# Second level of Strassen's algorithm in the first GEMM of a retention and ELU kernel, with sums taken into evacuations and twenty sums a block on GpSimd

## The chip, the cores and the metric

The kernel runs on one core of a Trainium2 chip. The metric is the device time of one execution in microseconds (us). A profile is of one execution, and its span is about 2 us below the time of that same execution. The profiled execution of the kernel before took 660.89 us, 2.8 us less than its median. Engines in the profile are PE (TensorE), PEld (its weight loads), DVE (VectorE), ACT (ScalarE), POOL (GpSimd) and SP (SyncE). Tiles lie in SBUF; TensorE's products are written to banks of PSUM, and an evacuation takes a result out of PSUM.

## The reference, cut to what matters

```python
# retention: 4 sequences of 768 tokens, 8 heads of 64; cut: k, v, decay
y = retention(q, k, v)                           # 3072 tokens x 512
h = x @ w_in                                     # 512 -> 2048: the first GEMM
g = np.where(h > 0.0, h, np.exp(np.minimum(h, 0.0)) - 1.0)   # ELU
out = g @ w_out                                  # 2048 -> 512: the second GEMM
```

Everything is float32. The 3072 tokens are done in six blocks of 512, counted from 0. While the second GEMM of one block runs, the retention of the next block is computed beside it.

## The kernel before

Strassen's algorithm (in Winograd's form) replaces the eight products of a 2x2 block multiplication by seven, at the price of sums of blocks. One level of it, as it is written in this kernel:

```python
    def strassen(product, use, between):
        # (cut: the yields, at which the caller interleaves other work)
        pa = bank("a")
        product(1, pa, True)
        m1 = kept(pa)                       # an evacuation from PSUM to SBUF
        pb = bank("b")
        product(2, pb, True)
        use("C11", plus(pb, m1))
        product(6, pa, False)               # adds to what stands in pa
        u2 = kept(pa)
        pd = bank("d")
        product(7, pd, True)
        product(5, pa, False)
        u4 = kept(pa)
        use("C22", plus(pd, u4))
        product(3, pa, False)
        use("C12", pa)
        product(4, pd, False)
        use("C21", plus(pd, u2))
```

The first GEMM uses one level in each of four groups of columns of `w_in` (`first(n)`, 7 products of 256 columns each). Each of its results goes through the ELU: two activations on ScalarE into a tile `r`, then one instruction on VectorE. Behind it VectorE takes the sums T3 and T1, which are inputs of the second GEMM:

```python
    def elu(g, h):
        r = epool.tile([P, 512], FP32, name="r", tag="r")
        nc.scalar.activation(r, h, AF.Relu, scale=-1.0)
        nc.scalar.activation(r, r, AF.Exp, scale=-1.0)
        flush()
        later.append(lambda: nc.vector.scalar_tensor_tensor(g, r, -1.0, h, ALU.add, ALU.max))
    # in first(n), behind the ELU of C12:
                later.append(lambda: sub(mine("T3"), mine("C22"), mine("C12")))
                later.append(lambda: sub(mine("T1"), mine("C12"), mine("C11")))
```

The second GEMM has had two levels from block 2 on (`second_twice`): 49 products of 128 columns. Each of its seven outer products needs four input sums of 128x512, on VectorE:

```python
        def inputs(j):
            ...
            sub(t[:, 0], b12, b11)
            sub(t[:, 1], b22, t[:, 0])
            sub(t[:, 2], b22, b12)
            sub(t[:, 3], b21, t[:, 1])
```

`ts` in the profile is a tile of such sums, `gC` and `gT` are quarters of the ELU's results and their sums, `wq` is the ring of small weights for the second level, and `res` holds the results of one inner product of the second GEMM.

## Time and profile before

| | before |
|---|---|
| time, median of 4 runs | 663.67 us (661.65 to 663.89) |
| span of the profiled run | 658.9 us |
| TensorE busy, clock granted | 637.3 us (97%), 1.000 |
| VectorE busy | 434.7 us (66%) |
| GpSimd busy | 23.8 us (4%) |
| start of block 2; blocks 2, 3, 4; block 5 to the end | 251.6; 101.65, 102.66, 102.87; 100.1 us |

### The profile page before, as it was taken

The page shows a single profiled execution, that of the slowest core. Times are in us where ns is not written, and L with a number is a line of the kernel's source. Part 1 is how long each engine was busy: PE and PEld are TensorE (multiplying, and loading weights), DVE is VectorE, ACT ScalarE, POOL GpSimd, SP SyncE. Part 2 cuts the span into 40 slices and gives each one's busy share as a digit, 9 for nine tenths or more (in the row PEclk, how much of TensorE's full clock was granted, in tenths as well). Part 3 has the DMA queues.
Part 4 walks back from the last instruction along what each step waited for, and adds up shares of the span by engine and source line. Part 5 has one row for each costly group of instructions (what it writes and reads, how often), then busy time and mean ns, then how long its engine had stood idle before and what let it go on. Part 6 is the DMA issues. An engine that isn't in the chain of part 4 may idle for free.

```text
span 658.9 us, 14662 instructions
## 1 busy us (share of the span) xinstructions
PE 637.3 (97%) x6144; PEld 537.5 (82%) x6144; DVE 434.7 (66%) x769; ACT 228.3 (35%) x432; POOL 23.8 (4%) x28
## 2 busy tenths in 40 slices
PE   4799999999999999999999999999999999999997
PEld 4664445458888888889999889999889999888996
DVE  5798688566757644549856457867447958355974
ACT  7477542014431002543112554111455111445211
POOL 1000100001100000200000200000100000000000
PEclk9999999999999999999999999999999999999999
DMA  8658977549114757605767703777801768200693
GB/s 342 235 166 289 343 228 232 143 133 376 72 65 160 255 211 257 254 1 174 223 206 254 251 1 95 228 228 253 301 2 42 242 206 267 96 1 20 222 305 126
DMA packets 63825, 123.64 MB, mean 188 GB/s; under 512 B 5136, under 2 KB 22544, under 8 KB 61712
## 3 DMA queue, kind: packets, MB, share of 16 engines
q1 hardware_dynamic: 63760, 122.70, 55.6%
q8 instruction: 49, 0.80, 0.5%
q14 instruction: 16, 0.13, 0.1%
HBM read 100.66 MB, written 22.02 MB: 186 GB/s over the span
## 4 chain that ended last, share of the span: by engine, by line
PE 95%; DVE 2%; DMA 1%; issue 1%; SPq 0%; ACT 0%; DVEq 0%
PE pa L497 21%; PE pa L618 15%; PE pd L497 10%; PE pd L618 8%; PE hp L396 6%; PE pb L497 5%; PE pa L410 4%; PE pa L555 4%; PE pb L618 4%; PE pd L555 2%; PE kv L287 2%; PE pb L410 2%; PE pd L410 2%; PE y L335 2%; PE sc L265 2%; PE y L311 2%
## 5 line engine op out<-in xcount | busy, mean ns | idle before, releaser
L452 DVE TENSOR_TENSOR h<-pd,m 128x512 f32<-128x512 f32 x42 | 29.1, 692 | 86.1 <-ACT m L447 68.6
L447 ACT COPY m<-pa 128x512 f32<-128x512 f32 x63 | 36.3, 577 | 109.7 <-PE pa L497 73.7
L626 ACT COPY ms<-pa 128x128 f32<-128x128 f32 x84 | 22.3, 265 | 125.3 <-PE pa L618 122.3
L374 ACT ACTIVATE r<-r 128x512 f32<-128x512 f32 x96 | 60.5, 630 | 3.0
L618 PE MATMUL pd<-ts,wq 128*128 128x128 f32 x448 | 59.9, 277 | 0.3 <-DVE res L630 0.3
L618 PE MATMUL pa<-ts,wq 128*128 128x128 f32 x448 | 59.2, 275 | 0.0
L373 ACT ACTIVATE r<-h 128x512 f32<-128x512 f32 x60 | 37.9, 631 | 57.2 <-DVE h L452 57.2
L618 PEld LDWEIGHTS pd<-ts,wq 128*128 128x128 f32 x448 | 54.5, 192 | 1.2 <-DVE res L630 0.9
L618 PEld LDWEIGHTS pa<-ts,wq 128*128 128x128 f32 x448 | 54.8, 192 | 0.2
L618 PE MATMUL pa<-gC,wq 128*128 128x128 f32 x384 | 52.0, 278 | 0.4 <-ACT ms L626 0.4
L376 DVE SCALAR_TENSOR_TENSOR gC<-r,h 128x512 f32<-128x512 f32 x60 | 42.1, 701 | 11.3 <-ACT r L374 11.3
L618 PEld LDWEIGHTS pa<-gC,wq 128*128 128x128 f32 x384 | 47.2, 192 | 1.7 <-ACT ms L626 0.5
L239 POOL TENSOR_TENSOR kvn<-kvn,vf 128x512 f32<-128x512 f32 x20 | 21.8, 1089 | 455.7 <-DMA kvn<-in_qkv_dram 455.7
L497 PE MATMUL pa<-xb,w_s 128*128 128x256 f32 x160 | 37.8, 379 | 0.0
L497 PE MATMUL pa<-xb,w_a 128*128 128x256 f32 x160 | 37.8, 379 | 0.0
L497 PE MATMUL pa<-xt,w_s 128*128 128x256 f32 x160 | 37.8, 379 | 0.0
L497 PE MATMUL pb<-xb,w_a 128*128 128x256 f32 x160 | 37.8, 379 | 0.0
L497 PE MATMUL pd<-xt,w_s 128*128 128x256 f32 x160 | 37.8, 379 | 0.0
L497 PE MATMUL pa<-xt,w_b 128*128 128x256 f32 x160 | 37.8, 379 | 0.0
L497 PE MATMUL pd<-xt,w_b 128*128 128x256 f32 x160 | 37.8, 379 | 0.0
L630 DVE TENSOR_TENSOR res<-pd,ms 128x128 f32<-128x128 f32 x56 | 16.1, 287 | 28.8 <-PE pd L618 26.3
L497 PEld LDWEIGHTS pb<-xb,w_a 128*128 128x128 f32 x160 | 30.4, 190 | 4.1
(121 smaller groups left out, 1092.7 us busy)
## 6 DMA issues: line engine op xcount, KB each, us to landing
wq<-scratch_dram SPq DMA_DIRECT2D x196, 256.0 KB, 4.0
wraw<-in_w_dram SPq DMA_DIRECT2D x16, 1024.0 KB, 6.0
qk<-in_qkv_dram SPq DMA_DIRECT2D x24, 512.0 KB, 8.7
kvn<-in_qkv_dram SPq DMA_DIRECT2D x24, 512.0 KB, 9.4
scratch_dram<-so SPq DMA_DIRECT2D x22, 512.0 KB, 3.4
ws<-scratch_dram SPq DMA_DIRECT2D x7, 1024.0 KB, 7.0
scratch_dram<-w_s SPq DMA_DIRECT2D x8, 512.0 KB, 7.3
out_dram<-res SPq DMA_DIRECT2D x12, 256.0 KB, 3.4
```

The costliest lines, as they stand in the source:

```text
L239: eng.tensor_tensor(out=kv[:, 1], in0=kv[:, 1], in1=vf[:, i].unsqueeze(2).to_broadcast([C, H, D]), op=ALU.mult)
L373: nc.scalar.activation(r, h, AF.Relu, scale=-1.0)
L374: nc.scalar.activation(r, r, AF.Exp, scale=-1.0)
L376: later.append(lambda: nc.vector.scalar_tensor_tensor(g, r, -1.0, h, ALU.add, ALU.max))
L396: nc.tensor.matmul(hp, lhsT=w[n][:, fi, j // 2, j % 2, :], rhs=xb[:, j, :], start=(j == 0), stop=(j == 3))
L410: nc.tensor.matmul(ops[d], lhsT=wo[:, row, d * P : (d + 1) * P], rhs=g_plain[row * NF + f], start=(f == 0 and row == 0), stop=(f == NF - 1 ...
L447: nc.scalar.copy(m, ps)
L452: nc.vector.tensor_tensor(out=h, in0=ps, in1=m, op=ALU.add)
L497: nc.tensor.matmul(ps[:, fi, :], lhsT=w[:, fi, j2, :], rhs=x[:, j2, :], start=(begin and fi == 0 and j2 == 0), stop=(j2 == 1), skip_group_ ...
L555: nc.tensor.matmul(ps[:, d, :], lhsT=ws[:, 2 * d + f // 4, f % 4, :], rhs=gq[INPUT2[j]][:, f, :], start=(begin and f == 0 and d == 0), sto ...
L618: nc.tensor.matmul(ps, lhsT=w[:, f, :], rhs=ts[j][k][:, f, :], start=(begin and f == 0), stop=(f == 3), skip_group_check=True,)
L626: nc.scalar.copy(m, ps)
```

## The change

The change gives the first GEMM a second level too, in blocks 2 to 5: 4 x 7 products of 256 columns become 7 x 7 products of 128, which is 49/56 of the arithmetic. Its price is more sums. To hold that down, the outer sums are taken along in the inner evacuations (`lift` adds the `addend`, `plus` writes to the destination), and 20 sums of 128x512 a block go to GpSimd: C22, C21 and T3 in four quarters each, the input sums of the second GEMM's first product, and T1 in four quarters. In the texts below j is the number of an outer product of the first GEMM, and product 1.6 is product 6 within outer product 1 of the second. The core of the diff, with cuts marked by `...`:

```diff
-    def elu(g, h):
+    def elu(g, h, depth=1, then=None):
-        r = epool.tile([P, 512], FP32, name="r", tag="r")
+        r = epool.tile([P, 512], FP32, name="r", tag="r", bufs=3)
...
+        def last():
+            nc.vector.scalar_tensor_tensor(g, e, -1.0, h, ALU.add, ALU.max)
+            if then:
+                then()
+        while len(later) >= depth:
+            later.pop(0)()
+        later.append(last)
...
+    PLAN = {
+        1: (None, "T3"), 2: ("T3", "C11"), 6: ("T3", "T3"), 5: ("T3", "C12"), 7: (None, "C21"),
+        3: ("C12", "C12"), 4: ("C21", "C21"),
+    }
+    def first_twice(tb, j):
+        addend, dst = PLAN[j]
...
+        def lift(ps, r, t, o=None):
...
+            if addend:
+                nc.vector.tensor_tensor(out=o, in0=ps, in1=place(addend, r, t), op=ALU.add)
+            else:
+                nc.scalar.copy(o, ps)
+            return o
+        def plus(r, t, ps, m):
+            nc.vector.tensor_tensor(out=place(dst, r, t), in0=ps, in1=m, op=ALU.add)
+        def done(r, t):
+            p = lambda name: place(name, r, t)
+            pool = lambda o, x, y, op: nc.gpsimd.tensor_tensor(out=p(o), in0=p(x), in1=p(y), op=op)
+            if j == 2:
+                elu(p("C11"), p("C11"), 2)
+            elif j == 7:
+                pool("C22", "C12", "C21", ALU.add)
+                pool("C21", "T3", "C21", ALU.add)
+                held_elu.append(lambda: elu(p("C22"), p("C22"), 2))
+            elif j == 3:
+                elu(p("C12"), p("C12"), 2, lambda: pool("T3", "C22", "C12", ALU.subtract))
+            elif j == 4:
+                held_elu.append(lambda: elu(p("C21"), p("C21"), 2))
...
-        inputs(1)
+        inputs(1, nc.gpsimd)
...
+    def combine_x_twice(part):      # the quarter sums of the first GEMM's input, on VectorE
...
+    for tb in range(2, NTB):        # (cut: the interleaving of first_twice and second_twice)
...
+                sec = second_twice(tb, lambda: (combine_x_twice(0), combine_x()) if more else None)
...
+        for n in range(4):
+            nc.gpsimd.tensor_tensor(out=place("T1"), in0=place("C12"), in1=place("C11"), op=ALU.subtract)
```

## The prediction

> **What bounds the kernel now.** I read the page's first two parts, then a table of stretches, then the groups of matmuls by shape, the chain that ended last, and for the disputed part the order of time.
>
> ```profile
> PE 637.3 (97%) x6144; PEld 537.5 (82%) x6144; DVE 434.7 (66%) x769; ACT 228.3 (35%) x432; POOL 23.8 (4%) x28
> PEclk9999999999999999999999999999999999999999
> PE 95%; DVE 2%; DMA 1%; issue 1%; SPq 0%; ACT 0%; DVEq 0%
> ```
>
> TensorE is the bound: busy 97% of the span, 95% of the chain that ended last, clock never throttled. VectorE (DVE) is second at 66%, GpSimd (POOL) nearly unused. So only fewer TensorE cycles can shorten the kernel, and whatever makes TensorE wait lengthens it at once.
>
> ```profile
> 303.80:355.80 52.00, 50.67 (x853) 49.17 (x852) 40.41 (x83) 8.10 (x28) 0.00 (x0) 1.00 0.74 234
> 355.80:400.00 44.20, 44.20 (x214) 39.11 (x214) 19.70 (x30) 21.30 (x37) 4.49 (x4) 1.00 0.36 126
> 400.00:452.00 52.00, 51.05 (x838) 49.52 (x837) 41.20 (x82) 10.89 (x32) 0.00 (x0) 1.00 0.68 210
> 349.50:452.40 102.90, 101.95 (x1101) 95.05 (x1100) 66.49 (x124) 33.57 (x73) 4.49 (x4) 1.00 0.55 178
> ```
>
> Columns: stretch in us, length, then busy us of PE, PEld, DVE, ACT, POOL. One block of 512 tokens takes 102.9 us. In the first GEMM (355.8 to 400) TensorE never stops and DVE is busy 45%. In the second GEMM with retention TensorE stands still for about 1 us a block, and DVE is busy 78%.
>
> ```profile
> L497 PE MATMUL pa<-xb,w_s 128*128 128x256 f32 x160 | 37.8, 379 | 0.0
> L618 PE MATMUL pa<-gC,wq 128*128 128x128 f32 x384 | 52.0, 278 | 0.4 <-ACT ms L626 0.4
> 286.29 1.73 PE pb L497 x8
> 303.84 1.79 PE pa L618 x16
> ```
>
> Means of pipelined matmuls overlap, so I take the pitch from the chain (start, length, what): a one-level product of 8 records with 256 columns takes 1.727 us, a two-level product of 8 records with 128 columns takes 1.79/2 = 0.89 us. Halving the columns costs only 3.6% over half.
>
> **What the skill says.** "TensorE: Matmul & The Clock Gate", section "Wait — 56ns, not 53.3ns?": start to start is N/2.4 GHz plus about 2.5 ns. A record here takes twice that (fp32): 0.216 and 0.111 us, against 0.218 and 0.112 worked out from it. It agrees: the smaller products pay almost no fixed cost.
>
> "VectorE: DVE Perf Modes", section on the TRN2 errata: an fp32 add of N elements takes (N+151)/0.96 ns, 691 for 512. The trace has 0.69 us, and back to back starts are 0.61 us apart (415.12, 415.73, 416.33). I count 0.61.
>
> "GPSIMD Engine Reference", section "Performance versus the Vector engine": about half of VectorE's speed on two-input elementwise work. Here the median of the 128x512 multiply is 1.04 us, 1.5 times 0.69.
>
> "SBUF — State Buffer", section "Who interferes with whom": a VectorE instruction with two SBUF inputs and a GpSimd instruction that reads SBUF exclude each other for a whole instruction; with at most one SBUF input they do not. The trace shows each case:
>
> ```profile
> 161.40 0.69 DVE L452 TENSOR_TENSOR h<-pd,m 128x512 f32<-128x512 f32 x1 [0.64 <-PE pd L497]
> ...
> 163.44 0.69 DVE L509 TENSOR_TENSOR gC<-gC,gC 128x512 f32<-128x512 f32 x1
> 163.50 1.53 POOL L239 TENSOR_TENSOR kvn<-kvn,vf 128x512 f32<-128x512 f32 x1 [1.52 <-DMA kvn<-in_qkv_dram]
> 164.05 1.53 DVE L431 TENSOR_TENSOR w_s<-w_a,w_b 128x512 f32<-128x512 f32 x1
> ...
> 268.23 1.04 POOL L239 TENSOR_TENSOR kvn<-kvn,vf 128x512 f32<-128x512 f32 x1 [97.38 <-DMA kvn<-in_qkv_dram]
> 268.66 1.16 DVE L509 TENSOR_TENSOR gT<-gC,gC 128x512 f32<-128x512 f32 x1
> ```
>
> An evacuation (one operand in PSUM) keeps its 0.69 beside a GpSimd operation that began at 160.94. GpSimd behind a VectorE sum is stretched to 1.53; a VectorE sum behind GpSimd to 1.53 and 1.16, ending 0.55 after it. So where both have work, they alternate at about 1.04 + 0.55 = 1.6 us per pair.
>
> **The change, part by part.**
>
> *TensorE, blocks 2 to 5.* First GEMM before: 4 column groups x 7 products x 1.727 = 48.4 us. After: 7 x 7 products x 0.89 = 43.6. Gain 4.75 us a block, 19.0 in four blocks, all of it on the path. The second GEMM keeps its products.
>
> *VectorE, first GEMM of a block.* Before: 12 evacuating sums, 16 ELU ends, 8 sums for T1 and T3: 36 x 0.61 = 22 us in 48.4. After: each of 49 products is evacuated at full width, 41 on VectorE (the addend is taken along) and 8 as ScalarE copies; with 16 ELU ends and 4 quarter sums of the input, 61 x 0.61 = 37 us in 43.6, or 85% before any exclusion. It fits on average but not everywhere. The built order of instructions gives, per inner product of 7 x 0.89 = 6.2 us, 9 operations for j=6, 7 for j=5, 6 for j=7, 10 for j=3 and 11 for j=4: 6.1 and 6.7 us in the last two. Those are where the exclusion falls, because:
>
> *GpSimd, per block.* Before 4 multiplies. After 24 operations: 4 multiplies, 12 sums for C22, C21 and T3, 4 input sums of the second GEMM's first product, 4 for T1. Twenty of these, 21 us alone, queue up from the end of j=7 to the second product of the second GEMM; 8 ELU ends on VectorE stand in the last two periods and, by then, have both inputs in SBUF. I assume 0.5 us lost to each: 4 us of VectorE time, of which some 1.5 meet slack.
>
> *New waits of TensorE, by laying the built order out with those durations from the start of a block (slots of 0.89):*
> (a) start of the block, 8 half-size input sums (about 0.35 each, from 128x256 at 0.42) and 8 full ones ahead of evacuations: 0.3.
> (b) j=3 and j=4: VectorE falls behind by some 2.5 us; the banks and the accumulation on the same bank allow 1 to 1.8 us: TensorE waits 1 to 2.
> (c) change to the second GEMM: product 1.6 needs the second GpSimd input sum. It stands behind two T3 sums that wait for ELU ends just after the last C12 evacuation. That is 4 x 1.04 + 0.55 after about slot 50, near 49.0, where TensorE arrives at 47.2: wait 1.8, up to 2.7 with the delays of (b).
> (d) product 2's input sums on VectorE alternate with T1 on GpSimd at 1.6 instead of 0.61: 0 to 2.3.
> Sum 3 to 7, central 3.75 (I lean low, since delays in (b) give GpSimd time to catch up and (d) has 2 us of slack unless both slip); the 1.0 of before falls away: +2.75 a block, +11 in four.
>
> *Once, block 1 to 2.* The first block with two levels needs its small weights at once. Their ring lies in memory that the last big weights occupied:
>
> ```profile
> 244.59 7.17 PE L555 MATMUL pd<-gC,ws 128*128 128x256 f32 x32
> 252.95 0.87 SPq L594 DMA_DIRECT2D wq<-scratch_dram  x2
> ```
>
> Before, that ring is loaded at 252.95 behind the last big product, with 48 us to spare. Now product 1.6 needs it 2 products after 251.7, at 253.5; with 2.5 to 4 us to landing (the page has a median of 4.0) it waits about 2. The 12 input sums (5.3 us) stand ahead of the evacuation that frees the bank of the next block's second inner product: another 2. With 1 us for the 28 GpSimd sums of the weights beside VectorE in block 1: +5.
>
> Sum: 663.9 - 19.0 + 11 + 5 = 661.
>
> **The rivals.**
> *Clean fit:* PSUM keeps TensorE ahead of evacuations, and the exclusion costs slack only. For it: VectorE at 85% fits on average, evacuations do not take part in the exclusion, two banks for pa and ELU ends held back by two. Then only (a), (c) and the once-only part remain: 663.9 - 19 + 4 x 1 + 4 = 653.
> *The exclusion binds:* every ELU end and input sum alternates with GpSimd. For it: the pairs above, and 20 GpSimd operations in 21 us against a change that wants their results in order. My layout taken strictly gives 8 us of waits a block: 663.9 - 19 + 28 + 6 = 679.
> *Weights late:* the ring of 11 now serves both GEMMs. Against it: 28 of 49 weights are fetched in the first GEMM (the products 1, 2 and 4 take theirs from SBUF), 28 x 256 KB = 7.3 MB in 44 us, 167 GB/s, below the 234 of the second GEMM, which goes without waiting for them. At most 2 us.
> *ScalarE binds:* 40 operations at 0.61 in the first GEMM, 24 us of 44, bunched at its end; it adds 0.8 in (c), hidden by GpSimd's wait.
>
> **Range and chances.** The saving is firm to 0.5 us; the waits run from 653 to 679, and contention has many small slacks that I can't follow. I take 661, 8 in 10 within 647 to 677. The 2% line is 650.6 below and 677.1 above. The first needs nearly all waits away: 0.18. The second needs the strict alternation and more once-only cost: 0.14. Within 2%: 0.68.
>
> **What would show it.** Right: products of 0.89 in the first GEMM; block period near 101; DVE busy 80% or more there; GpSimd busy without gaps at the change of GEMMs, ELU ends and input sums there well over 0.69; waits of TensorE in j=3, j=4 and product 1.6 of 3 to 4 us a block; a single gap of about 4 us near 253 to 261. Wrong: pitch above 0.89 or gaps behind weight DMAs (rival three); no stretched VectorE sums (rival one); the first GEMM as long as before, 48 us, with TensorE waiting on VectorE throughout (rival two, worse than I think).

## More of the kernel before

For the comparison with the changed kernel, here is block 4 cut into stretches: the first two are most of the first GEMM, the third is its end and the change to the second GEMM, and the last is the second GEMM with retention. Columns: stretch, its length, then busy us (and instructions) of PE, PEld, DVE, ACT and POOL, the granted clock, the DMA share and GB/s.

```profile
455.90:482.00 26.10, 26.10 (x131) 23.21 (x130) 11.01 (x18) 11.60 (x21) 4.17 (x4) 1.00 0.69 241
482.00:500.00 18.00, 18.00 (x85) 15.84 (x84) 10.24 (x16) 10.44 (x18) 0.00 (x0) 1.00 0.00 0
500.00:521.00 21.00, 21.00 (x270) 20.00 (x269) 17.62 (x33) 6.36 (x16) 0.00 (x0) 1.00 0.49 152
521.00:558.80 37.80, 36.65 (x634) 35.77 (x634) 28.07 (x60) 4.79 (x18) 0.00 (x0) 1.00 0.76 234
```

TensorE is busy in every microsecond of the change of GEMMs (21.00 of 21.00), though VectorE is already busy for 17.62 of 21 us there. GpSimd does nothing in it.

The input sums of the second GEMM are worth noting for later (columns: line, engine, operation, tiles, shapes, count, busy us, mean ns):

```profile
L607 DVE TENSOR_TENSOR ts<-gC,ts 128x512 f32<-128x512 f32 x48 | 33.0, 688 | 0.8
```

## The result, and the profile after

The changed kernel took 710.33 us (median of 4 runs, 708.59 to 711.38), and the kernel before beside it 663.67 us. The ratio is 1.0708, with a 95% interval of 1.0677 to 1.0738: slower by 7%, far above the predicted 661 and outside 647 to 677. A ratio is always the mean time of one kernel's fast runs over that of the other's fast runs of the same rounds, so it is not quite the ratio of the medians quoted.

The page after, first the busy line, the clock's row and the chain that ended last:

```profile
PE 641.2 (91%) x6816; PEld 556.2 (79%) x6816; DVE 552.9 (78%) x885; ACT 221.6 (31%) x416; POOL 188.9 (27%) x136
...
PEclk9999999999999989999999999999999999999999
...
PE 62%; DVE 15%; POOL 11%; issue 5%; DMA 4%; ACT 1%; SPq 0%; DVEq 0%; POOLq 0%
```

TensorE was 95% of the chain that ended last and is 62% now; VectorE and GpSimd make up 26%. TensorE is even busy for longer than before, 641.2 us, although its first GEMM has an eighth less to do in four of the six blocks. The clock's row hides why: a slice is 18 us long, and the drops to half clock last 3 to 4 us. The stretches of block 4 show them (same columns as before):

```profile
493.80:520.00 26.20, 26.20 (x233) 25.94 (x231) 19.16 (x30) 8.85 (x15) 4.62 (x4) 1.00 0.93 320
520.00:536.00 16.00, 13.96 (x117) 13.14 (x116) 15.76 (x22) 8.51 (x15) 13.17 (x9) 1.00 0.58 170
536.00:557.00 21.00, 15.09 (x120) 14.13 (x123) 17.77 (x22) 7.21 (x17) 17.44 (x11) 0.92 0.54 167
```

Over the first 26 us nothing is wrong: TensorE is full. Once GpSimd has work (13.17 of 16 us, then 17.44 of 21), TensorE loses 2.0 and then 5.9 us, and the clock falls to a mean of 0.92. The same stretch of the kernel before was full. The order of time on TensorE names the waits (start, length, engine, line, what, and in brackets the idle time before it and what ended that):

```profile
531.61 1.16 PE L696 MATMUL pa<-ts,wq 128*128 128x128 f32 x8 [1.60 <-DVE m L707]
...
542.64 1.52 PE L769 MATMUL pa<-ts,wq 128*128 128x128 f32 x8 [3.08 <-POOL ts L647]
544.31 2.07 PE L769 MATMUL pd<-ts,wq 128*128 128x128 f32 x8 [0.15 <-POOL ts L647]
...
554.86 1.16 PE L769 MATMUL pd<-ts,wq 128*128 128x128 f32 x8 [2.56 <-DVE res L781]
...
603.15 1.16 PE L769 MATMUL pd<-ts,wq 128*128 128x128 f32 x8 [1.72 <-DVE res L781]
```

A product of 8 records is 1.06 to 1.16 us long when the clock is full. Behind the wait of 3.08 us it is 1.52 and 2.07: TensorE runs at half clock. Behind the wait of 2.56 us it is 1.16, so not every long wait is followed by half clock. VectorE and GpSimd at the wait of 2.56 us:

```profile
547.57 6.29 POOL L1027 TENSOR_TENSOR gC<-gC,gC 128x512 f32<-128x512 f32 x4
549.43 1.64 DVE L647 TENSOR_TENSOR ts<-gC,ts 128x512 f32<-128x512 f32 x1
550.99 1.75 DVE L647 TENSOR_TENSOR ts<-gC 128x512 f32<-128x512 f32 x1
552.66 1.74 DVE L647 TENSOR_TENSOR ts<-gC,ts 128x512 f32<-128x512 f32 x1
```

Four sums on GpSimd take 6.29 us, and beside them VectorE's input sums take 1.64 to 1.75 us each, where they took 0.688. They start about 1.6 us apart: one on each engine in turn. The `res` addition that TensorE waits for stands behind them. The groups show how far this reaches:

```profile
L382 DVE SCALAR_TENSOR_TENSOR gC<-r,gC 128x512 f32<-128x512 f32 x64 | 67.2, 1064 | 3.3 <-ACT r L379 3.3
...
L647 DVE TENSOR_TENSOR ts<-gC,ts 128x512 f32<-128x512 f32 x40 | 35.6, 889 | 0.7
```

Where the time went, by the starts of the blocks in the profiled runs (a third kernel is put beside the two, with the 20 GpSimd sums left out; it is told under the experiments):

| us | before | after | sums left out |
|---|---|---|---|
| up to the start of block 2 | 251.6 | 255.8 | 255.7 |
| block 2 | 101.65 | 117.37 | 104.55 |
| block 3 | 102.66 | 113.10 | 101.82 |
| block 4 | 102.87 | 112.31 | 101.56 |
| block 5 to the end | 100.1 | 109.5 | 98.9 |
| span | 658.9 | 708.1 | 662.5 |

### The profile page after: what moved, and what is told of

Its sections match the earlier page's. It is cut to its first block, busy times and chain, and to the rows that moved or that the text cites. A ratio compares the mean times of both kernels' runs of the same rounds, so it can differ in the third digit from the quotient of the medians.

```text
span 708.1 us, 16611 instructions
## 1 busy us (share of the span) xinstructions
PE 641.2 (91%) x6816; PEld 556.2 (79%) x6816; DVE 552.9 (78%) x885; ACT 221.6 (31%) x416; POOL 188.9 (27%) x136
## 4 chain that ended last, share of the span: by engine, by line
PE 62%; DVE 15%; POOL 11%; issue 5%; DMA 4%; ACT 1%; SPq 0%; DVEq 0%; POOLq 0%
PE pa L769 9%; PE pa L696 8%; PE pd L769 6%; PE hp L408 6%; DVE ts L647 6%; POOL gC L717 4%; PE pa L567 4%; PE pa L422 4%; PE pe L696 4%; POOL wi L636 2%; POOL ts L647 2%; PE pd L567 2%; DVE res L781 2%; PE pd L422 2%; PE pb L422 2%
## 5 line engine op out<-in xcount | busy, mean ns | idle before, releaser
L769 PE MATMUL pa<-ts,wq 128*128 128x128 f32 x448 | 63.0, 286 | 12.9 <-POOL ts L647 12.3
L696 PE MATMUL pa<-ts,wq 128*128 128x128 f32 x448 | 62.4, 284 | 11.5 <-DVE m L707 7.9
L382 DVE SCALAR_TENSOR_TENSOR gC<-r,gC 128x512 f32<-128x512 f32 x64 | 67.2, 1064 | 3.3 <-ACT r L379 3.3
L769 PEld LDWEIGHTS pa<-ts,wq 128*128 128x128 f32 x448 | 57.6, 201 | 14.1 <-POOL ts L647 13.1
L696 PEld LDWEIGHTS pa<-ts,wq 128*128 128x128 f32 x448 | 56.1, 197 | 13.8 <-DVE m L707 10.0
L378 ACT ACTIVATE r<-gC 128x512 f32<-128x512 f32 x64 | 40.1, 627 | 60.9 <-DVE gC L713 27.2
L647 DVE TENSOR_TENSOR ts<-gC,ts 128x512 f32<-128x512 f32 x40 | 35.6, 889 | 0.7
L647 DVE TENSOR_TENSOR ts<-gC 128x512 f32<-128x512 f32 x40 | 34.1, 852 | 0.0
L422 PE MATMUL pa<-gC,w_s 128*128 128x512 f32 x64 | 30.6, 600 | 0.0
L696 PE MATMUL pe<-ts,wq 128*128 128x128 f32 x224 | 30.6, 281 | 0.0
L567 PE MATMUL pa<-gC,ws 128*128 128x256 f32 x128 | 28.7, 382 | 1.7 <-DMA ws<-scratch_dram 1.7
L709 ACT COPY m<-pa 128x512 f32<-128x512 f32 x16 | 9.4, 585 | 60.6 <-PE pa L696 60.6
```

What stands on the lines that cost most here:

```text
L378: nc.scalar.activation(e, h, AF.Relu, scale=-1.0)
L382: nc.vector.scalar_tensor_tensor(g, e, -1.0, h, ALU.add, ALU.max)
L422: nc.tensor.matmul(ops[d], lhsT=wo[:, row, d * P : (d + 1) * P], rhs=g_plain[row * NF + f], start=(f == 0 and row == 0), stop=(f == NF - 1 ...
L567: nc.tensor.matmul(ps[:, d, :], lhsT=ws[:, 2 * d + f // 4, f % 4, :], rhs=gq[INPUT2[j]][:, f, :], start=(begin and f == 0 and d == 0), sto ...
L647: sub = lambda o, x, y: eng.tensor_tensor(out=o, in0=x, in1=y, op=ALU.subtract)
L696: nc.tensor.matmul(ps[:, f, :], lhsT=lhs[f], rhs=xs[j][k], start=(begin and f == 0), stop=True, skip_group_check=True,)
```

## The experiments

Theory X after the result: a GpSimd sum and a VectorE instruction with two operands in SBUF exclude each other, and the 20 sums stand where VectorE is nearly full, so VectorE falls behind and TensorE waits. The rivals: VectorE has too much to do by itself (V); the results of GpSimd come late, because each sum is long and the order is bad (L); and the half clock behind a wait is a cost of its own (C), which may join any of them. In the expectations "theory E" stands for the exclusion together with single bad places in the order.

**1. The sums on VectorE.**

```diff
-            pool = lambda o, x, y, op: nc.gpsimd.tensor_tensor(out=p(o), in0=p(x), in1=p(y), op=op)
+            pool = lambda o, x, y, op: nc.vector.tensor_tensor(out=p(o), in0=p(x), in1=p(y), op=op)
-        inputs(1, nc.gpsimd)
+        inputs(1)
```

T1 was moved likewise.

> The 20 sums that the change gave to GpSimd in each of four blocks go to VectorE; the result stays right. Theory E (VectorE and GpSimd exclude each other[...], and this stretches VectorE and delays the sums): VectorE's ELU ends fall back from 1.06 to 0.69 us, the sums from 1.27-1.7 us to 0.61, and although VectorE gets 20 x 0.61 = 12 us more of its own per block, the kernel gets faster: about 690 us, from 710. Rival V (VectorE simply has too much to do, GpSimd relieves it): slower than 710, about 720 to 735.

Measured: 712.08 us (709.66 to 713.41), ratio 1.072 [1.0664, 1.0777], as slow as the change. Theory E expected some 690 and missed; the rival expected 720 to 735 and missed too. VectorE's instructions have their old length again:

```profile
L382 DVE SCALAR_TENSOR_TENSOR gC<-r,gC 128x512 f32<-128x512 f32 x64 | 43.4, 688 | 1.6 <-ACT r L379 1.6
```

and yet VectorE is busy for longer, 569.2 us against 552.9, since it does 80 sums more. Moving them to GpSimd relieved it by only 16 us. So the run does not refute the exclusion; it shows that putting the sums on either engine costs about the same.

**2. The ELU's `r` in PSUM**, so that its last instruction has only one operand in SBUF.

```diff
-        r = epool.tile([P, 512], FP32, name="r", tag="r", bufs=3)
+        if depth == 2:
+            r = ps_r.tile([P, 512], FP32, name="rp", tag="r")
+        else:
+            r = epool.tile([P, 512], FP32, name="r", tag="r", bufs=3)
...
-        pd = full(ps_r.tile([P, 2, TH], FP32, name="pe", tag="r"))
+        pd = full(bank("d"))
```

> ELU's exponential is left in PSUM, so that the 16 ELU ends per block have one operand in SBUF instead of two; nothing else changes, the result stays right. Theory E: ELU ends at 0.69 us beside a busy GpSimd, GpSimd's own sums nearer 1.27 than 1.65, TensorE's waits for VectorE in the products of j=3 and j=4 (2.0 us a block) and for GpSimd's input sum (3.1 us) shrink: 15 to 25 us faster than 710. Rival V: the same number of VectorE operations, so within 5 us of 710. Rival D (order of dependent GpSimd sums alone): the 3.1 us wait stays at 2.5 or more, under 8 us gained.

The second hunk frees the PSUM bank that `r` takes, so one product accumulates in another bank than in the change.

Measured: 698.5 us (695.8 to 699.39), ratio 1.0511 [1.0465, 1.0558], so 12 us faster than the change, where 15 to 25 had been expected.

```profile
L385 DVE SCALAR_TENSOR_TENSOR gC<-rp,gC 128x512 f32<-128x512 f32 x64 | 42.7, 683 | 7.2 <-ACT rp L382 7.2
L650 DVE TENSOR_TENSOR ts<-gC 128x512 f32<-128x512 f32 x40 | 35.2, 880 | 0.0
...
L720 POOL TENSOR_TENSOR gT<-gC,gC 128x512 f32<-128x512 f32 x16 | 20.2, 1275 | 10.2 <-DVE gC L385 10.2
```

The ELU ends are back at 683 ns although GpSimd works beside them as before, and the input sums, still with two operands in SBUF, stay at 880. GpSimd's sums beside the ELU ends are back at 1275 ns too, from 1566 in the change. The operand's memory decides whether an instruction is held up.

**3 to 5. The three bad places in the order, one at a time.** T1 taken from another formula during inner product 6 (run 3), T3 put behind the input sums in GpSimd's order (run 4), and the full-size input sums of the next block put behind that block's first products (run 5).

```diff
# 3
+            if j == 6:
+                for n in range(4):
+                    nc.gpsimd.tensor_tensor(out=place("T1"), in0=place("C22"), in1=place("C11"), op=ALU.subtract)
# 4
-                elu(p("C12"), p("C12"), 2, lambda: pool("T3", "C22", "C12", ALU.subtract))
+                elu(p("C12"), p("C12"), 2, lambda: held_t3.append(lambda: pool("T3", "C22", "C12", ALU.subtract)))
# 5
-                sec = second_twice(tb, lambda: (combine_x_twice(0), combine_x()) if more else None)
+                sec = second_twice(tb, lambda: combine_x_twice(0) if more else None)
...
             if at == 0 and tb > 2:
+                combine_x()
                 combine_x_twice(1)
```

> The four T1 sums on GpSimd are taken later, as C22 minus the next C11, out of the way of the input sums of the second product; same engine, same number, result right. If the wait of 2.6 us a block for VectorE (product 7 of the second inner product) comes from VectorE's input sums alternating with T1, it vanishes: 8 to 10 us faster, input sums at 0.69 there. If it comes from VectorE's backlog alone: under 3 us gained.

> GpSimd's input sums of the second GEMM's first product go ahead of the four T3 sums; same work on all engines, result right. If the 3.1 us wait comes from the T3 sums that stand in front in GpSimd's queue (2 x 1.65 us): the wait falls under 1 us and with it the stretch at half clock behind it, 12 to 20 us faster in four blocks, unless the T3 sums are then late for the next C11. If it comes from GpSimd's pace or from ScalarE's copy instead: under 5 us.

> The four full-size input sums of the next block are moved behind the first products of that block; same work, result right. The wait of 1.7 us a block for VectorE before product 4 of the last inner product (a sum that stands behind 12 input sums) should be gone or under 0.3: 5 to 7 us faster than 710 over the changes of block 3, 4 and 5. If that wait is only replaced by another one: under 2 us.

Measured: 708.72 us (706.69 to 711.34), 710.17 us (708.5 to 711.79) and 715.49 us (710.31 to 717.08). None gained anything that matters. The third has a median 5 us above the change's, but the interval of its ratio, 1.0685 to 1.0788, overlaps the change's. In each the wait aimed at was gone and others stood in its place. In run 3 the 2.56 us wait became this one, an inner product later:

```profile
446.78 1.57 PE L769 MATMUL pd<-ts,wq 128*128 128x128 f32 x8 [2.11 <-DVE res L781]
```

In run 4 the wait of 3.08 us for GpSimd's input sum dissolved into 0.57, 0.37, 0.33, 1.41 and 2.01 us for VectorE and for the issue of instructions. The reading that fits: when VectorE is behind by several microseconds, reordering moves the point at which TensorE notices it. Run 12 tests it.

**6. Runs 2, 3, 4 and 5 in one kernel.**

> ELU's exponential in PSUM, T1 late, GpSimd's input sums first, full-size input sums behind: all four at once, result right. Theory E ([...]each of these alone only hands the wait on to the next two-operand sum): together more than the sum of what they gave alone (12 + 2 + 0 + what the last gives): 676 to 686 us. Rival (each wait has its own cause): 12 + 2 + 0 + 6 = 20, about 690.

Measured: 691.47 us (690.92 to 693.79), ratio 1.0396 [1.0362, 1.043], nearer to the rival's number than to theory E's. Of the 19 us gained, run 2 alone had brought 12.

**7. As 6, with the once-only transition to block 2 mended:** the sums of the last large weights first, and only the half-size input sums ahead of the first products.

```diff
-        combine_x_twice(1)
...
-    cur = second(1, combine_x, change)
+    cur = second(1, lambda: None, change)
...
-            if at == 0 and tb > 2:
+            if at == 0:
```

> As the run before, and at the change from block 1 to 2 the sums of the last big weights and the half-size input sums come first, so that the small weights' loads are issued about 2.4 us earlier. If the once-only gap (3.6 us of waiting for a weight's transfer, products at half clock after it) hangs on that: 3 to 5 us faster than the four together. If the transfer itself is the limit: under 1.5.

Measured: 686.67 us (684.79 to 687.51), ratio 1.031 [1.0271, 1.0349]: 4.8 us faster, as expected. This is the fastest correct version of the change that was run, and it is still 3% slower than the kernel before.

**8. The kernel before, with GpSimd's sums added.** Nothing of the change but the company: 20 sums a block on an idle tile, in the kernel before.

```diff
+    idle = const.tile([P, TB], FP32, name="idle")
+    nc.gpsimd.memset(idle, 0.0)
...
+            if tb > 1:
+                for _ in range(5):
+                    nc.gpsimd.tensor_tensor(out=idle, in0=idle, in1=idle, op=ALU.add)
```

> The kernel BEFORE with 20 GpSimd sums of two SBUF operands (128x512, on a tile that nobody reads) in each of the last four blocks; result right. Theory E: VectorE's two-operand sums in the first GEMM are stretched, to 0.9 us or more on average there, but VectorE is busy only 45% there and TensorE does not wait: under 5 us slower than 663.7. If GpSimd's activity itself slows the kernel (transfers, clock): 10 us or more.

Measured: 675.43 us (672.93 to 677.42), ratio 1.0146 [1.0107, 1.0185]. That is 10 to 12 us more, so theory E's "under 5" was missed and the number lies in the rival's range. The blocks tell why. Block 3, where 20 sums happened to run within the first GEMM, took 102.9 us, 0.3 more than before. Block 2 did the same and took 103.5, 1.9 more, of which 1.6 are in one wait in the retention when GpSimd is idle. So GpSimd's activity by itself does not slow the kernel. Nothing gated the later sums, so 20 of them (19 in the line below) ran back to back across the change of GEMMs in block 4, and that block took 116.4 us, 13.5 more:

```profile
499.91 26.08 POOL L805 TENSOR_TENSOR idle<-idle 128x512 f32<-128x512 f32 x19
...
509.55 1.41 DVE L609 TENSOR_TENSOR ts<-gC,ts 128x512 f32<-128x512 f32 x1
...
515.95 1.16 PE L620 MATMUL pd<-ts,wq 128*128 128x128 f32 x8 [3.76 <-DVE h L454]
```

A dependency cannot be the reason, as nobody reads that tile. Twenty sums cost 0.3 us in one place and 13.5 us in another. Nor does it begin with the clock: in that block it halved only from 527.8 us on, and the product behind the wait of 3.76 us is 1.16 us long, at full clock.

**9. The change with the sums left out** (wrong results; TensorE, ScalarE and VectorE keep their work).

```diff
-            pool = lambda o, x, y, op: nc.gpsimd.tensor_tensor(out=p(o), in0=p(x), in1=p(y), op=op)
+            pool = lambda o, x, y, op: None
```

The four input sums were left out and their places in the products given to operands that exist; T1 was left out.

> The changed kernel with the 20 GpSimd sums of each block left out altogether (the results are wrong on purpose; TensorE, VectorE and ScalarE keep all their work). Theory E (GpSimd's sums, by their length and by what they keep VectorE from, make the waits): the two waits of 2.6 to 3.1 us at the change of GEMMs and the half clock behind them go, the wait for the evacuations shrinks; per block 3.25 + 3.1 + 2.0 + about 1 of the 12.9 us measured, times 4 = 37 us: 668 to 680. Rival V (VectorE's own share of the second level is too much by itself, GpSimd only adds to it): 690 or more, with TensorE waiting for VectorE where it waits for GpSimd now.

Measured: 665.04 us (664.16 to 667.63), ratio 1.0022 [0.9986, 1.0057]. So 45 us of the change's time hang on these 80 sums, more than expected, and rival V is out: VectorE's own share fits.

```profile
PE 629.6 (95%) x6816; PEld 548.1 (83%) x6816; DVE 514.5 (78%) x885; ACT 220.8 (33%) x416; POOL 65.3 (10%) x56
...
L382 DVE SCALAR_TENSOR_TENSOR gC<-r,gC 128x512 f32<-128x512 f32 x64 | 43.5, 696 | 1.7 <-ACT r L379 1.2
```

These lines price the sums. VectorE is busy 514.5 us instead of 552.9 with the very same 885 instructions: the 80 sums on GpSimd stretched VectorE's work by 38.4 us, or 0.48 us each. In run 1 the same sums on VectorE took it (569.2 - 514.5)/80 = 0.68 us each. And GpSimd needed (188.9 - 65.3)/80 = 1.55 us each.

Leaving the sums out also shows a limit: the change only draws level with the kernel before, even with these sums for nothing.

**10. Dummy matmuls in the waits** of the change, to keep TensorE from standing still; nobody reads their result.

```diff
+    def keep_busy(count, rhs):
+        idle = ps_r.tile([P, P], FP32, name="idle", tag="r")
+        for n in range(count):
+            nc.tensor.matmul(idle, lhsT=W_IN[1][:, 0, 0, 0, :], rhs=rhs, start=True, stop=True, skip_group_check=True)
...
+            if j == 1:
+                keep_busy(11, ts[1][1][:, 0, :])
             product(j, 6, pa, False)
...
+            if j == 2:
+                keep_busy(9, ts[2][1][:, 0, :])
             product(j, 7, pd, True)
...
+        if tb == 2 and j == 1:
+            keep_busy(14, xs[1][1])
         product(6, pa, False)
```

> The changed kernel with dummy matmuls whose result nobody reads, in the three waits that are over 2 us (11 of 0.22 us ahead of the product that waits for GpSimd's input sum, 9 ahead of the one that waits 2.56 us in each block, 14 in the wait for the first small weights), so that TensorE isn't idle in them. Theory C (the granted clock halves because TensorE stood still, and that costs 1.2 to 2 us a block more than the waits themselves): no 0.5 in the clock's row, the products behind these waits at a pitch of 0.89, 701 to 705. Rival: the time that TensorE loses at half clock is lost anyway, as VectorE is behind and the next wait absorbs it: 708 to 712, with the clock full and the later waits longer.

Measured: 699.59 us (698.11 to 701.65), ratio 1.0537 [1.0495, 1.0579]; the results are correct. It is 10.7 us faster than the change, a little more than theory C expected, by work that nobody needs:

```profile
531.91 2.62 PE L760 MATMUL idle<-gC,w_a 128*128 128x128 f32 x22
535.17 1.16 PE L776 MATMUL pa<-ts,wq 128*128 128x128 f32 x8 [0.64 <-POOL ts L647]
536.85 1.16 PE L776 MATMUL pd<-ts,wq 128*128 128x128 f32 x8 [0.52 <-POOL ts L647]
```

The products behind the wait are 1.16 us long instead of 1.52 and 2.07. The waits themselves remain, filled. Half clock thus cost some 10.7 of the 46.7 us. The clock's record agrees: TensorE was at half clock for 23.9 us of blocks 2 to 5 in the change, which costs at most half of that, and never in run 10; block 2, with the longest wait, gained 5.0 of them (112.4 against 117.4).

**11. Run 7 with the sums left out** (wrong).

> The version with four repairs and the repaired transition (686.7), with GpSimd's 20 sums of each block left out (wrong on purpose). It bounds what any better placing of these sums could bring. Theory E: of the 4.3 us by which its blocks are longer than those of the kernel before, and of the 4.75 us that the shorter products should save, nearly all comes back: (4 + 4) times 3 to 4 blocks less about 1 us a block of VectorE's own waits = 24 less: 657 to 668. Rival V: 675 or more, the change can't win even with the sums for nothing.

Measured: 676.9 us (674.46 to 679.52), ratio 1.0194 [1.0149, 1.024]. A miss for theory E, and in rival V's range. But V is not the cause, as run 9 also has the sums left out and takes 665: with the repairs the kernel is 12 us slower than without them. Its blocks 3 and 4 take 105.65 and 106.03 us against 101.82 and 101.56. The largest new wait comes with the repair of run 5:

```profile
476.00 1.26 PE L699 MATMUL pa<-ts,wq 128*128 128x128 f32 x8 [2.16 <-DVE m L710]
477.39 2.08 PE L699 MATMUL pd<-ts,wq 128*128 128x128 f32 x8
```

These lines are of run 11, and run 7 has the same wait, also of 2.16 us, with half clock behind it in both: the input sums, moved behind the first products, delay the evacuation that frees `pa`. So runs 6 and 7 carry one repair that harms. How much of the 12 us it costs was not measured: a version of run 7 without it, and with dummy matmuls, was not run.

**12. The sums at their places, but nobody reads them** (wrong). As run 9, with GpSimd's 20 sums of each block put back, with their own operands, writing to an idle tile. The tile takes the memory of one of the eleven slots of small weights.

```diff
+    idle = const.tile([P, 4, P], FP32, name="idle")
-    RING = 11
+    RING = 10
-            pool = lambda o, x, y, op: nc.gpsimd.tensor_tensor(out=p(o), in0=p(x), in1=p(y), op=op)
+            pool = lambda o, x, y, op: nc.gpsimd.tensor_tensor(out=idle, in0=p(x), in1=p(y), op=op)
...
-            nc.gpsimd.tensor_tensor(out=place("T1"), in0=place("C12"), in1=place("C11"), op=ALU.subtract)
+            nc.gpsimd.tensor_tensor(out=idle, in0=place("C12"), in1=place("C11"), op=ALU.subtract)
```

> As the run with the sums left out (665.0), but with GpSimd's 20 sums of each block back at their places and with their own operands, and their results written to an idle tile that nobody reads (wrong on purpose; the idle tile takes the memory of one of the 11 slots of the small weights). So nobody waits for a result of GpSimd, but GpSimd occupies its memory access as in the change. Theory X (the sums cost by keeping VectorE's instructions with two operands in memory from theirs): VectorE's ELU ends at 1.0 us and input sums at 0.85 to 0.9 us mean as in the change, TensorE waits for VectorE, and most of the 45 us stays: 690 to 705. Rival L (the sums cost because their results come late): 665 to 675, whatever VectorE's durations are.

Measured: 711.75 us (710.27 to 713.04), ratio 1.0725 [1.0688, 1.0762]. This is the time of the change itself, above even theory X's range, and rival L is out. No engine waits for a result of these sums, nor for GpSimd to have read its operands, and the whole 45 us are there. (That the two times are so close is chance: this run stands at half clock for 34.1 us in blocks 2 to 5, the change for 23.9.)

```profile
PE 66%; DVE 20%; issue 5%; ACT 3%; DMA 3%; POOL 2%; SPq 0%; DVEq 0%
...
L383 DVE SCALAR_TENSOR_TENSOR gC<-r,gC 128x512 f32<-128x512 f32 x64 | 71.9, 1142 | 0.0
```

GpSimd's share of the chain fell from 11% to 2% and VectorE's rose from 15% to 20%; the ELU ends are as stretched as before. So the wait of 3.08 us that the profile put down to GpSimd was not the cause: without it, the time goes into waits for VectorE at the same change of GEMMs. This fits runs 3 and 4, which removed such waits and gained nothing. The one slot less is not the reason: the list of all waits of this run has none of TensorE for the ring of small weights. Four waits of 2.1 us, one a block, stand in it as "issue"; each ends 0.1 us after VectorE's second input sum of the second product (in block 4 the sum ends at 550.50 and the product starts at 550.61), so they are waits for VectorE as well. The wait at the start of block 2 is as long as in the change (3.58 against 3.60 us).

## Why the prediction was wrong

Its own steps, in order:

- *TensorE's saving.* Right in kind, a quarter too large. The bare pitch was 0.89 us, but some starts stand 0.95 to 1.0 us apart, above all at the head of an inner product. In run 9, where TensorE has no wait in the first GEMM of block 4, its 49 products take 44.67 us from start to start, against 48.36 for the 28 before: 3.7 us a block, not the 4.75 that were called firm to 0.5. They were saved, and then more than given back.
- *What bounds the kernel, and where the trouble would be.* Right in place: GpSimd without gaps at the change of GEMMs, stretched ELU ends and input sums, and waits in j=3, j=4, product 1.6 and product 2.
- *"I assume 0.5 us lost to each: 4 us of VectorE time, of which some 1.5 meet slack."* **This term failed.** Run 9 against the change puts VectorE's loss at 38.4/4 = 9.6 us a block. I counted 8 ELU ends and 4 us; the groups of the change against run 9 show (67.2 - 43.5)/4 = 5.9 us a block lost on the 16 ELU ends (11 of the 16 in block 4 took over 0.75 us), and 3.7 on the input sums, which I had only as "0 to 2.3" under (d). There was little slack: with the sums left out, VectorE is busy for 29.45 of 32 us at this place (run 9, 496 to 528 us).
- *GpSimd's 20 operations "21 us alone".* Sized from the wrong form. The 1.04 us was a multiplication of the old kernel. A sum of the change takes 1.27 us where VectorE does not hold it up (1275 ns in run 2), and 1.55 on average in the change: 31 us a block. What makes the 1.27 is not shown: run 8's sum of a whole tile with itself also takes 1.04 undisturbed, while the sums of the change work on quarters of tiles.
- *The four waits, "Sum 3 to 7, central 3.75 (I lean low ...)".* This is where the wrong term entered the total. Block 4 had (a) 1.9 instead of 0.3, (b) 2.7 instead of 1 to 2, (c) 3.25 instead of 1.8 to 2.7 and (d) 3.1 instead of 0 to 2.3, each measured as the excess of the starts over the normal pitch: 10.9 us together. The leaning low was wrong in kind: delays in one place did not give others time to catch up. When a wait was taken away another came (runs 3 and 4), and VectorE fell as far behind with nobody waiting for GpSimd (run 12). Nor did "the 1.0 of before" fall away: the wait of 1.15 us in the retention of block 4 is still there (1.14).
- *(a) apart.* The product that waits 1.7 us there needs the `res` addition of the previous inner product, which stands on VectorE behind the 12 input sums. I saw those sums ahead of the evacuations of the new block and overlooked this addition. The wait is the same with GpSimd's sums left out (1.73 us in run 9), so it belongs to the order and not to the exclusion.
- *The clock.* Absent from the prediction, though it read that the clock had never been throttled before. Behind some of the waits TensorE ran at half clock (behind all four of 3.08 us, but only one of the four of 2.56): 2.0 us in block 4, and 10.7 us in all by run 10. With it, the waits of block 4 cost 12.9 us instead of 3.75. Less the 3.7 saved, that is 9.2 of the 9.4 us by which the block grew.
- *Once-only: +5.* Too low. Run 9, which has no sums, is 4.1 us later at the start of block 2 and 2.9 us longer in it, 7 us together (2.2 of the 4.1 are there at the start of block 1 already, where the profiles of all runs lie between 145.65 and 148.84 us, so part may be chance); the change adds some 1.5 to 2 more in block 2 than in the later blocks (117.37 - 104.55 = 12.8 against 10.6 to 11.3).
- *The rivals.* "The exclusion binds" was the right mechanism, with 8 us of waits a block for a measured 10.9, and no half clock. "Clean fit" at 653 was out of reach even with the sums for nothing (665). "Weights late" and "ScalarE binds" did not occur apart from the one wait for weights at the start of block 2.

Together: the prediction had -19 + 11 + 5 = -3 us. The profiled runs have +4.2 at the start of block 2, then +15.7, +10.4, +9.4 and +9.4, which is +49.

What stays open: whether a version with the useful repairs alone, with (a) mended and with TensorE kept busy, comes near the kernel before. Run 9 makes it unlikely that it would win by much, as it gets the sums for nothing, but it still pays (a) and the start of block 2.

## What to carry to other kernels

Before moving elementwise sums to GpSimd, look at what VectorE does at that very place: beside VectorE instructions with two SBUF operands, a sum moved here still cost VectorE 0.48 of the 0.68 us that doing it took, while in a stretch where VectorE had room 20 sums cost TensorE 0.3 us (run 8, block 3). When removing a wait gains nothing and another appears, stop reordering; leave the suspected work out, then put it back with nobody reading it, and the two runs tell whether its results or its presence cost. Where half clock follows a wait of TensorE, cheap matmuls in that wait can keep the clock (10.7 us in run 10).

## What the Trainium skill lacked or had wrong

- "SBUF — State Buffer", section "Who interferes with whom": its rule held in runs 2, 8 and 12. An ELU end with both operands in SBUF took 1.06 us on average beside GpSimd and 0.68 with one operand in PSUM (run 2). What it lacks is the price: alternating pairs at 1.6 to 1.75 us, and a VectorE that keeps paying 0.48 us for each 128x512 sum moved away.
- "GPSIMD Engine Reference", section "3.1 Elementwise — side-by-side cycle accounting": it measures an addition at one size, 2048 elements, 1.96 times VectorE's time. At 512 the sums of the change have 1.275 us undisturbed (run 2) against 0.688, 1.85 times, but run 8's sum of a whole tile with itself 1.04, 1.5 times. The section has no second operand shape to compare with, and the runs leave open what makes the difference.
- "TensorE: Matmul & The Clock Gate", section "Why this matters for your kernels": it advises against idle gaps of more than about 3 us. Here half clock followed waits of 2.16 us as well (a product of 2.08 us behind one in run 11, normal 1.06), and did not follow one of 3.76 us (run 8, a product of 1.16). That useless matmuls in a wait pay (10.7 us in run 10) is shown by the runs.
